# Crossing from a tiled attention-and-MoE front to a second MoE: the norm's steps and the last tile's scaling put ahead of side work, and the side steps of a quad's products dealt out by a table

## The chip, the core and the metric

One core of a Trainium2 chip runs the whole program in one launch. The metric is the device time of that core in microseconds (us); lower is better. The engines are TensorE (PE, with its weight loads shown apart as PEld), VectorE (DVE), ScalarE (ACT), GpSimd (POOL) and SyncE (SP), which only issues DMAs here. Each engine works through its own queue in order; semaphores let it wait for the others.

## What is computed

Three stages follow each other, all in fp32:

```
kv = einsum('bhsd,bhse->bhde', k, v);  out = einsum('bhsd,bhde->bhse', q, kv)   # B=4, H=8, S=576, D=64
x  = out / rms(out) * g_norm                       -> x [2304, 512]
h  = x @ w_in [512, 1024];  solu = h * softmax(h);  ln = (solu - mean) / std * g_ln
x  = ln @ w_out [1024, 512]                                                     # first MoE
y  = ((x @ w_a [512, 1536]) * (x @ w_b)) @ w_out2 [1536, 512]                   # second MoE
```

## The kernel before

**Front part.** The 2304 tokens are 18 tiles of 128. For a tile `i` the first MoE runs these steps: `hp` (24 matmuls into `ph`), `hm` (maximum, DVE), `he` (exponential, ACT), `hs` (SoLU, DVE, line 461), `hq` (squares, ACT, line 469), `hn` (the norm: a small tensor `nmu` on POOL, nine 128x1 steps on DVE from line 478 on, and for the last two tiles the scaling of `so` on ACT, line 486), `lt`/`lh`/`ll` (transposes on PE, line 495; their high part on ACT and low part on DVE), `yp`/`yk` (the product with `w_out`, 24 matmuls into `x2p`, and its copy by ACT to DRAM, `x2d`). The order is written out by hand in strings such as `LATER`, and `run(...)` emits it.

**Every fp32 operand is split** into a high and a low part (ACT casts the high part, DVE or POOL subtracts for the low part), and each product takes three matmuls: high by high, low by high, high by low.

**Second MoE.** Its tokens are three blocks `s` of 768, its hidden width six steps `j`, with `m` = 0 for `w_a` and `m` = 1 for `w_b`. `quad(j, s, m)` makes one 2x2 block product by seven smaller products (a Strassen-like scheme) in three PSUM banks, each product six matmuls of 384 columns. In the order of PE: the first (bank b1; ACT copies it out), the second (b2; DVE adds it into `22`, line 761), the third (b3; DVE adds it into `12`, line 765), then the last product of the quad before (`close_quad`), the fourth (b1), the fifth (b2) and the sixth (b3). The fifth may not write b2 before line 761 has read it, the sixth not b3 before line 765 has. After the fifth, the sixth and the closing product DVE adds once more (line 740); the closing product waits until the sixth product's add has read b3. With `m` = 1 the result is multiplied by that of `m` = 0 (line 751, mostly on POOL) and sent to DRAM (`gd`).

**Side work.** Operands for later quads are prepared between the products. `quad` takes a list `side` of steps, and after the first, second, third, fourth, fifth and sixth product `tick` emits some of them; before, `ceil(steps left / ticks left)` each time. `w_narrow` has ten steps (the absolute values on ACT, a clamp for each half on DVE, line 67, shifts, signs, lows, the next fetch), `w_sums` four (POOL or DVE), `w_split` four (cast, subtract, cast, subtract), `w2_sums` five, `x_steps` its casts and subtractions. In the last step `j` = 5 the quads run in the order of s = 1, 2, 0, and further steps (`then(t1=..., t6=...)`) are emitted at named ticks, after the side steps of that tick: loads of `gd` into `ga`, `te` and `gw`, loads of the last weights (`wo`), and their splits (`half`, `g_first`). After these come nine `out_pair` calls, the last matrix product.

**The crossing.** Tile 16 runs `LATER` with the first quad's operand splits (`side`, from `x_split`) put in between; tile 17 follows by hand. `w_split(0)` makes the first weight operands, `quad(0, 0, 0)` runs, then tile 17's transposes, the last `y_product` calls, and `quad(0, 0, 1)`. `w_sums(1)` runs on POOL.

Of the kernel before, what the change touches and what calls it, by code (L numbers as in the profile page):

```python
# [41 lines left out]
hp hm xt+1 op+2 lt0-1 lt1-1 lh0-1 lh1-1 ll0-1 ll1-1 xh+1 xl+1 he os+2 yp yk hs hq om+2 kp kk qt+3  # L42
qk+3 LQ yp yk hn MM E E BP BP ox+2 LK
"""


def split(nc, hi, lo, src, eng=None):
# [53 lines left out]
def tile_attention_moe(ctx, tc, q, k, v, g_norm, w_in, w_out, g_ln, w_a, w_b, w_out2, out):  # L101
    nc = tc.nc
# [442 lines left out]
    WA11, WA12, WS3, WA22, WS1, WS2, WS4 = range(7)  # L545
    XB11, XT1, XT2, XB21, XB22, XT3, XT4 = range(7)
# [178 lines left out]
    def quad(j, s, m, side=()):  # L725

        w, x = ws2[2 * j + m], xs2[s]
        side = list(side)
        ticks = [6]

        def tick():

            for _ in range(-(-len(side) // ticks[0])):
                side.pop(0)()
            for f in delayed.pop(7 - ticks[0], ()):
                f()
            ticks[0] -= 1

        def add(t, ps):
            nc.vector.tensor_tensor(out=t, in0=ps, in1=t, op=ALU.add)  # L740

        if m == 0:
            a_of[j, s] = {
                n: p2["a"].tile([P, TH], F32, tag=f"a{n}", name=f"a{n}") for n in (11, 12, 21, 22)
            }
        a = a_of[j, s]
        t = a if m == 0 else {n: p2["b"].tile([P, TH], F32, tag=f"b{n}", name=f"b{n}") for n in (12, 21, 22)}

        def times(n, by, eng):

            eng.tensor_tensor(out=a[n], in0=by, in1=a[n], op=ALU.mult)  # L751
            at_ = (11, 12, 21, 22).index(n)
            nc.sync.dma_start(out=gd[s][:, at_, :, j], in_=a[n].rearrange("p (m t) -> p m t", t=P))

        b1 = bank()
        product(b1, w, x, WA11, XB11, True, False)
        nc.scalar.copy(t[21], b1)
        tick()
        b2 = bank()
        product(b2, w, x, WS1, XT1, True, False)  # L760
        nc.vector.tensor_tensor(out=t[22], in0=b2, in1=t[21], op=ALU.add)  # L761
        tick()
        b3 = bank()
        product(b3, w, x, WS2, XT2, True, False)
        nc.vector.tensor_tensor(out=t[12], in0=b3, in1=t[21], op=ALU.add)
        close_quad()
        tick()
        product(b1, w, x, WA12, XB21, False, True)
        if m == 0:
            nc.scalar.copy(a[11], b1)  # L770
        else:
            times(11, b1, nc.vector)
        tick()
        product(b2, w, x, WS4, XB22, False, True)
        add(t[12], b2)
        if m:
            times(12, t[12], nc.gpsimd)
        tick()
        product(b3, w, x, WS3, XT3, False, False)
        add(t[22], b3)  # L780
        if m:
            times(22, t[22], nc.gpsimd)
        tick()

        def close():
            product(b3, w, x, WA22, XT4, False, True)
            add(t[21], b3)
            if m:
                times(21, t[21], nc.vector if (j, s) == (NJ - 1, 0) else nc.gpsimd)

        open_quad.append(close)
# [197 lines left out]
    def load_gl(_):  # L989
# [10 lines left out]
        lt0=lambda i: l_turn(i, 0), lt1=lambda i: l_turn(i, 1),  # L1000
        lh0=lambda i: l_hi(i, 0), lh1=lambda i: l_hi(i, 1),
        ll0=lambda i: l_lo(i, 0), ll1=lambda i: l_lo(i, 1),
# [3 lines left out]
    def run(order, i=0):  # L1006
        for token in order.split():
            name, _, at_ = token.replace("-", "+-").partition("+")
            if 0 <= i + int(at_ or 0) < NTILE:
                acts[name](i + int(at_ or 0))  # L1010
# [8 lines left out]
    def all_of(steps):  # L1019
        for f in steps:  # L1020
            f()
# [25 lines left out]
    i = NTILE - 2  # L1047
    side = [f for n in ORDER for f in x_split(0, n, lambda n=n: xf[n])]
    at_ = LATER.split().index("hn")
    run(" ".join(LATER.split()[:at_]), i)  # L1050
    all_of(side[:2])
    run("hn", i)
    all_of(w_sums(0))
    all_of(side[2:8])
    run(" ".join(LATER.split()[at_ + 1:]), i)
# [10 lines left out]
    p2["a"] = pool_r("a", 2, ab)  # L1066
    p2["b"] = pool_r("b", 1, ab)
    run("lt0-1 lt1-1 lh0-1 lh1-1 ll0-1 ll1-1", i)
    all_of(w_split(0, nc.vector))
    all_of(side[10:])  # L1070
    run("hs", i)
    while pend:
        y_product(0)
        y_keep(0)
    banks["pool"] = ps_t
    xf, sums = x_begin(1)
    quad(0, 0, 0, [lambda: run("hq", i), lambda: None, lambda: run("hn", i)])
    run("lt0 lt1 lh0 lh1 ll0 ll1", i)
    all_of(w_sums(1))
    all_of(sums)  # L1080
    all_of(w_split(1, nc.vector))
# [83 lines left out]
    def wl(n, place_, i, eng=nc.sync):  # L1165
        return lambda: wo_load(n, *place_[2 * i:2 * i + 2], eng)

    def half(n, part, eng=nc.vector):
        return hi_lo(wo2, n, eng, part)

    def gl_(n, c):
        return lambda: g_load(0, n, c, te[:, 2] if n == XT3 else None)
# [15 lines left out]
    for n, k in ((XB11, 0), (XT1, 1)):  # L1188
# [2 lines left out]
    most, last = slice(0, NJ - 1), slice(NJ - 1, NJ)  # L1191
    early, late_ = g_first(most), g_first(last)
    then(
        t1=[gl_(XB11, most), gl_(XT3, most)], t4=[gl_(XB22, most), gl_(XB21, most)], t6=early[:3],
    )
    quad(j, 1, 0)
    then(t1=early[3:4], t2=early[4:6], t3=early[6:7], t4=early[7:8], t5=early[8:10])
# [3 lines left out]
    )  # L1201
    quad(j, 2, 0)
    then(
        t2=half(WA11, 0), t3=[wl(WS2, w1, 2), *late_[:4]], t4=half(WA11, 1), t5=late_[4:8], t6=late_[8:],
    )
    quad(j, 2, 1)
    then(
        t1=half(WS1, 0), t2=half(WS1, 1), t3=[second_place], t4=[wl(WA12, w2, 0, nc.scalar), *half(WS2, 0)],
        t5=[wl(WS4, w2, 1, nc.scalar), *half(WS2, 1)], t6=[wl(WS3, w2, 2, nc.scalar), *g_split(0, XT2, lambda: te[:, 1])],
    )  # L1210
    quad(j, 0, 0)
# [39 lines left out]
    side = []  # L1251
# [49 lines left out]
```

## Time and profile before

| | us |
|---|---|
| median of three runs (lowest, highest) | 700.51 (699.49, 701.65) |
| the profiled execution's own time | 702.19 |
| its span in the trace | 700.1 |
| PE busy in the span | 665.7 |
| DVE, POOL, ACT busy | 519.6, 302.8, 284.1 |

The span is what the trace covers; the rest of the execution's time (2.1 us) lies around it. Times in rows are counted from the span's start. The front part lasts until about 283, the quads from there to about 572, the `out_pair` calls to the end.

### The profile page before, as it was taken

How to read it: one execution, taken by the hardware profiler on the slowest of the kernel's cores; microseconds unless marked ns; L12 is line 12 of the kernel's file. 1: busy time of each engine (PE TensorE's matmuls, PEld its weight loads, DVE VectorE, ACT ScalarE, POOL GpSimd, SP SyncE). 2: the span in 40 equal slices, each digit the busy share in tenths (PEclk: the TensorE clock that was granted, in tenths of full speed). 3: DMA queues.
4: the chain of work that ended last, by engine and by line, in shares of the span. 5: the costliest groups of instructions: out<-in, count | busy, mean ns of one | idle time of the engine just before them, and what ended most of it. 6: DMA issues, size and time to landing. Idle time of an engine off the chain costs nothing.

```text
span 700.1 us, 12578 instructions
## 1 busy us (share of the span) xinstructions
PE 665.7 (95%) x4710; PEld 633.0 (90%) x4710; DVE 519.6 (74%) x930; ACT 284.1 (41%) x491; POOL 302.8 (43%) x446
## 2 busy tenths in 40 slices
PE   1699999999999999999999999999999999999998
PEld 1577798999999998899999999999998899999998
DVE  3889977676688776779656867577656779987883
ACT  2558854544455346543331122212212445443431
POOL 2588776677666311113654467444672140000000
PEclk9899999999999999999999999999999999999999
DMA  9998645645542502342344336544334694654521
GB/s 248 316 248 234 184 127 156 168 127 149 178 127 76 167 16 68 106 136 81 111 149 136 118 106 187 177 136 142 112 95 129 221 313 139 190 146 130 150 76 61
DMA packets 107132, 103.84 MB, mean 148 GB/s; under 512 B 25280, under 2 KB 94400, under 8 KB 107072
## 3 DMA queue, kind: packets, MB, share of 16 engines
q1 hardware_dynamic: 101024, 94.40, 46.3%
q10 hardware_dynamic: 6048, 8.65, 3.7%
q8 instruction: 37, 0.61, 0.4%
q14 instruction: 23, 0.19, 0.1%
HBM read 71.05 MB, written 31.98 MB: 147 GB/s over the span
## 4 chain that ended last, share of the span: by engine, by line
PE 76%; DVE 9%; issue 5%; POOL 4%; DMA 3%; ACT 1%; SPq 1%; DVEq 0%; ACTq 0%; POOLq 0%
PE pw L710 26%; PE pq L881 18%; PE x2p L527 5%; PE x2p L525 5%; PE x2p L526 5%; PE ph L438 4%; PE ph L440 4%; PE ph L439 4%; PE ltp L495 2%; PE po L376 2%; DMA vs<-in_v_dram 1%; POOL a L751 1%; DMA wo<-w2d 1%; DMA gw<-gd 1%; PE xtp L413 1%
## 5 line engine op out<-in xcount | busy, mean ns | idle before, releaser
L751 POOL TENSOR_TENSOR a<-b,a 128x384 f32<-128x384 f32 x53 | 63.3, 1208 | 127.2 <-DVE b L740 126.2
L710 PE MATMUL pw<-xh,wh 128*128 128x384 f32 x336 | 114.3, 340 | 2.6 <-DVE b L761 1.6
L710 PE MATMUL pw<-xh,wl 128*128 128x384 f32 x336 | 112.7, 335 | 0.0
L710 PE MATMUL pw<-xl,wh 128*128 128x384 f32 x336 | 112.6, 335 | 0.0
L710 PE MATMUL pw<-x,wh 128*128 128x384 f32 x336 | 85.8, 336 | 0.9 <-DVE b L740 0.6
L525 PE MATMUL x2p<-lh,woh 128*128 128x256 f32 x288 | 82.6, 287 | 0.3 <-ACT lh L505 0.2
L526 PE MATMUL x2p<-ll,woh 128*128 128x256 f32 x288 | 80.6, 280 | 0.8 <-DVE ll L508 0.8
L527 PE MATMUL x2p<-lh,wol 128*128 128x256 f32 x288 | 80.6, 280 | 0.5 <-DVE wol L50 0.5
L710 PEld LDWEIGHTS pw<-xh,wh 128*128 128x128 f32 x336 | 63.1, 188 | 7.1 <-DVE b L761 2.3
L710 PEld LDWEIGHTS pw<-xl,wh 128*128 128x128 f32 x336 | 63.1, 188 | 0.0
L710 PEld LDWEIGHTS pw<-xh,wl 128*128 128x128 f32 x336 | 63.1, 188 | 0.0
L710 PEld LDWEIGHTS pw<-x,wh 128*128 128x128 f32 x336 | 60.5, 188 | 1.8 <-DVE b L740 0.9
L438 PE MATMUL ph<-wih,xh 128*128 128x512 f32 x144 | 56.9, 395 | 0.8 <-DVE so L461 0.8
L881 PE MATMUL pq<-wo,gh 128*128 128x256 f32 x336 | 57.7, 276 | 0.0
L440 PE MATMUL ph<-wih,xl 128*128 128x512 f32 x144 | 56.3, 391 | 1.2 <-DVE xl L423 1.2
L439 PE MATMUL ph<-wil,xh 128*128 128x512 f32 x144 | 56.3, 391 | 0.4 <-DVE wil L50 0.4
L710 PE MATMUL pw<-x,wl 128*128 128x384 f32 x168 | 56.2, 335 | 0.0
L527 PEld LDWEIGHTS x2p<-lh,wol 128*128 128x128 f32 x288 | 54.6, 190 | 0.9 <-DVE wol L50 0.9
L526 PEld LDWEIGHTS x2p<-ll,woh 128*128 128x128 f32 x288 | 54.2, 188 | 1.2 <-DVE ll L508 1.2
L525 PEld LDWEIGHTS x2p<-lh,woh 128*128 128x128 f32 x288 | 54.2, 188 | 0.9 <-ACT lh L505 0.5
L881 PE MATMUL pq<-wo,gw 128*128 128x256 f32 x450 | 53.1, 276 | 0.0
L67 POOL TENSOR_SCALAR nu<-nu 128x512 f32<-128x512 f32 x23 | 44.7, 1955 | 17.1 <-ACT nu L62 16.1
(158 smaller groups left out, 1536.0 us busy)
## 6 DMA issues: line engine op xcount, KB each, us to landing
gd<-a SPq DMA_DIRECT2D x72, 192.0 KB, 2.0
ring<-in_moe_w_out_dram SPq DMA_DIRECT2D x20, 512.0 KB, 5.4
gl<-gd SPq DMA_DIRECT2D x14, 384.0 KB, 3.5
gw<-gd SPq DMA_DIRECT2D x12, 384.0 KB, 3.2
ring<-in_moe_w_in_dram SPq DMA_DIRECT2D x8, 512.0 KB, 7.3
qs<-in_q_dram SPq DMA_DIRECT2D x16, 256.0 KB, 6.5
x2d<-x2s ACTq DMA_DIRECT2D x32, 128.0 KB, 1.8
st<-in_moe_w_a_dram SPq DMA_DIRECT2D x8, 512.0 KB, 4.3
```

The source lines that it names most:

```text
L67: eng.tensor_scalar(out=u, in0=u, scalar1=2.0 ** -15, scalar2=122879.9921875, op0=ALU.max, op1=ALU.min)
L376: nc.tensor.matmul(po[a:a + n, 2 * hp:2 * hp + 2, :], qT[i][:, hp, a:a + n], kvb[b % 3][:, hp, :], start=True, stop=True,)
L438: nc.tensor.matmul(ph[:, n, :], xh[:, c, :], wh, start=(c == 0), stop=False)
L439: nc.tensor.matmul(ph[:, n, :], xh[:, c, :], wl, start=False, stop=False)
L440: nc.tensor.matmul(ph[:, n, :], xl[:, c, :], wh, start=False, stop=(c == NK - 1))
L495: nc.tensor.transpose(pt[:, m, :], hs_[i]["so"][:, f * P:(f + 1) * P], ident)
L525: nc.tensor.matmul(pa, wh[:, cs], lh[:, f, :], start=(f == 0), stop=False)
L526: nc.tensor.matmul(pa, wh[:, cs], ll[:, f, :], start=False, stop=False)
L527: nc.tensor.matmul(pa, wl[:, cs], lh[:, f, :], start=False, stop=(f == NF1 - 1))
L710: nc.tensor.matmul(out, wt_[:, wn, c], xt_[xn][:, c], start=first and c == n == 0, stop=c == 1 and n == 2, skip_group_check=not first,)
L751: eng.tensor_tensor(out=a[n], in0=by, in1=a[n], op=ALU.mult)
L881: nc.tensor.matmul(ps, xt_[:, c], wt_[:, c], start=first and c == n == 0, stop=c == NJ - 1 and n == 2, skip_group_check=not first,)
```

## The change

It has three parts.

First, in the crossing, tile 16's `hn` is emitted before the first operand split instead of behind it; tile 17's `hs` comes before `w_split(0)` and the last four operand splits instead of after them; its `hq` comes after the first of the remaining `yp yk` instead of after the first quad's first product; and its transposes and their splits come after the fifth product of `quad(0, 0, 0)` instead of after the whole quad.

Second, a table `DEAL` says for 13 kinds of quad, by (s, m, number of side steps), how many steps follow each of the six products.

Third, in the steps `then(...)` of the last `j`, some are moved by one tick.

```diff
+DEAL = {
+    (0, 0, 6): "121011",
+    (0, 1, 8): "312020",
...
+    (2, 1, 4): "111001",
+    (0, 0, 4): "102100",
+    (0, 1, 10): "113212",
+    (1, 0, 8): "321011",
+    (1, 1, 10): "033202",
...
         ticks = [6]
+        deal = DEAL.get((s, m, len(side)))
...
-            for _ in range(-(-len(side) // ticks[0])):
+            for _ in range(-(-len(side) // ticks[0]) if deal is None else int(deal[6 - ticks[0]])):
                 side.pop(0)()
...
     run(" ".join(LATER.split()[:at_]), i)
+    run("hn", i)
     all_of(side[:2])
-    run("hn", i)
     all_of(w_sums(0))
...
     run("lt0-1 lt1-1 lh0-1 lh1-1 ll0-1 ll1-1", i)
+    run("hs", i)
     all_of(w_split(0, nc.vector))
     all_of(side[10:])
-    run("hs", i)
+    run("yp yk hq", i)
     while pend:
...
-    quad(0, 0, 0, [lambda: run("hq", i), lambda: None, lambda: run("hn", i)])
-    run("lt0 lt1 lh0 lh1 ll0 ll1", i)
+    none = [lambda: None]
+    quad(0, 0, 0, [lambda: run("hn", i), *3 * none, lambda: run("lt0 lt1 lh0 lh1 ll0 ll1", i), *none])
     all_of(w_sums(1))
...
-        t1=[gl_(XB11, most), gl_(XT3, most)], t4=[gl_(XB22, most), gl_(XB21, most)], t6=early[:3],
+        t1=[gl_(XB11, most), gl_(XT3, most)], t3=[gl_(XB22, most), gl_(XB21, most)], t6=early[:3],
...
-        t2=half(WA11, 0), t3=[wl(WS2, w1, 2), *late_[:4]], t4=half(WA11, 1), t5=late_[4:8], t6=late_[8:],
+        t3=[wl(WS2, w1, 2), *half(WA11, 0), *late_[:4]], t4=[*half(WA11, 1), *late_[4:8]], t6=late_[8:],
...
-        t1=half(WS1, 0), t2=half(WS1, 1), t3=[second_place], t4=[wl(WA12, w2, 0, nc.scalar), *half(WS2, 0)],
+        t2=half(WS1, 0), t3=[second_place, *half(WS1, 1)], t4=[wl(WA12, w2, 0, nc.scalar), *half(WS2, 0)],
```

No instruction is added or taken away. The queues differ at these places above all.

DVE in the crossing, before: behind the last operand splits (`wl`, `xl`) come tile 17's SoLU (`rs`, `so`), then the first quad's adds of the second and third product (`a<-pw,a`), then the norm's small steps (`va` to `nmu`), the adds of the fifth and sixth product, and the low parts `ll` of the transposes.

```order
L552 TENSOR_TENSOR wl_3611<-w0s,wh_3610 128x768 [waits Activation_49]
L552 TENSOR_TENSOR xl_3385<-xf,xh_3378 128x768 [waits Activation_49]
L552 TENSOR_TENSOR xl_3386<-xf,xh_3379 128x768 [waits Activation_49]
L457 TENSOR_SCALAR rs<-se 128x1
L461 SCALAR_TENSOR_TENSOR so,su<-ph,rs,e 128x1024 [waits DVE_49]
L761 TENSOR_TENSOR a_3751<-pw,a_3750 128x384 [waits PE_49,Activation_49]
L765 TENSOR_TENSOR a_3749<-pw,a_3750 128x384 [waits PE_49]
L478 TENSOR_SCALAR va<-vs 128x1 [waits Activation_49]
L485 TENSOR_TENSOR nmu<-nmu,y_l 128x1 [waits DVE_49,Pool_49]
L740 TENSOR_TENSOR a_3749<-pw,a_3749 128x384 [waits PE_49]
L740 TENSOR_TENSOR a_3751<-pw,a_3751 128x384 [waits PE_49]
L508 TENSOR_TENSOR ll<-ltp,lh 128x4x128 [waits Activation_49] x2
```

The same place on DVE after the change (line numbers are 15 or 16 higher):

```order
L472 TENSOR_SCALAR rs<-se 128x1
L476 SCALAR_TENSOR_TENSOR so,su<-ph,rs,e 128x1024 [waits DVE_49]
L567 TENSOR_TENSOR wl_3617<-w0s,wh_3616 128x768 [waits Activation_49]
L567 TENSOR_TENSOR xl_3385<-xf,xh_3378 128x768 [waits Activation_49]
L567 TENSOR_TENSOR xl_3386<-xf,xh_3379 128x768 [waits Activation_49]
L493 TENSOR_SCALAR va<-vs 128x1 [waits Activation_49]
L500 TENSOR_TENSOR nmu<-nmu,y_l 128x1 [waits DVE_49,Pool_49]
L777 TENSOR_TENSOR a_3753<-pw,a_3752 128x384 [waits PE_49,Activation_49]
L781 TENSOR_TENSOR a_3751<-pw,a_3752 128x384 [waits PE_49]
L756 TENSOR_TENSOR a_3751<-pw,a_3751 128x384 [waits DVE_49,PE_49]
L523 TENSOR_TENSOR ll<-ltp,lh 128x4x128 [waits Activation_49] x2
L756 TENSOR_TENSOR a_3753<-pw,a_3753 128x384 [waits PE_49]
```

The SoLU moved ahead of the operand splits, the norm's steps ahead of the quad's first add, and the low parts ahead of the sixth product's add. On PE the eight transposes moved ahead of the sixth product, and nothing else there moved in the whole program.

DVE in `quad(1, 1, 1)`, before; `quad(j, 1, 1)` and `quad(j, 0, 1)` of j = 1 to 4 read alike. `b<-pw,b` of line 761 and 765 are the adds of the second and third product, line 740 the later adds, 67 to 93 the steps of `w_narrow`, 751 the multiplication of the fourth product.

```order
L67 TENSOR_SCALAR st<-st 128x512 [waits Activation_49]
L761 TENSOR_TENSOR b_4555<-pw,b_4554 128x384 [waits PE_49]
L67 TENSOR_SCALAR st<-st 128x512 [waits Activation_49]
L82 TENSOR_SCALAR st<-st 128x512 [waits DVE_49]
L765 TENSOR_TENSOR b_4553<-pw,b_4554 128x384 [waits PE_49]
L740 TENSOR_TENSOR a_4487<-pw,a_4487 128x384 [waits DMAHW4_49,PE_49]
...
L93 SCALAR_TENSOR_TENSOR st<-st 128x512 [waits DVE_49]
L740 TENSOR_TENSOR b_4553<-pw,b_4553 128x384 [waits PE_49]
L93 SCALAR_TENSOR_TENSOR st<-st 128x512 [waits DVE_49]
L740 TENSOR_TENSOR b_4555<-pw,b_4555 128x384 [waits PE_49]
```

After the change:

```order
L777 TENSOR_TENSOR b_4555<-pw,b_4554 128x384 [waits PE_49,Activation_49]
L82 TENSOR_SCALAR st<-st 128x512 [waits Activation_49] x2
L781 TENSOR_TENSOR b_4553<-pw,b_4554 128x384 [waits PE_49]
L756 TENSOR_TENSOR a_4487<-pw,a_4487 128x384 [waits DMAHW4_49,PE_49]
L97 TENSOR_SCALAR st<-st 128x512 [waits DVE_49] x2
...
L108 SCALAR_TENSOR_TENSOR st<-st 128x512 [waits DVE_49]
L756 TENSOR_TENSOR b_4553<-pw,b_4553 128x384 [waits PE_49]
L756 TENSOR_TENSOR b_4555<-pw,b_4555 128x384 [waits PE_49]
L108 SCALAR_TENSOR_TENSOR st<-st 128x512 [waits DVE_49]
```

The second product's add moved ahead of the first clamp, both clamps now stand ahead of the third product's add, the first shift behind it, and the last low behind the sixth product's add.

DVE in `quad(5, 2, 1)`, before (`wo`: the low part of a half of the weights `WA11`):

```order
L761 TENSOR_TENSOR b_6206<-pw,b_6205 128x384 [waits PE_49,Activation_49]
L552 TENSOR_TENSOR wo_6175<-wo_6175 128x768 [waits DMAHW3_49,Activation_49]
L765 TENSOR_TENSOR b_6204<-pw,b_6205 128x384 [waits PE_49]
L740 TENSOR_TENSOR a_6131<-pw,a_6131 128x384 [waits DMAHW4_49,PE_49]
L552 TENSOR_TENSOR te<-te,ga 128x128 [waits DMAHW5_49,DMAHW4_49]
```

After the change:

```order
L777 TENSOR_TENSOR b_6206<-pw,b_6205 128x384 [waits PE_49,Activation_49]
L781 TENSOR_TENSOR b_6204<-pw,b_6205 128x384 [waits PE_49]
L756 TENSOR_TENSOR a_6131<-pw,a_6131 128x384 [waits DMAHW4_49,PE_49]
L567 TENSOR_TENSOR wo_6175<-wo_6175 128x768 [waits DMAHW3_49,Activation_49]
L567 TENSOR_TENSOR te<-te,ga 128x128 [waits DMAHW5_49,DMAHW4_49]
```

The weights' subtraction moved behind two adds. On POOL, in `quad(j, 2, 1)`, the second subtraction of `w_split` moved behind the multiplications of the fifth and sixth product. SP's queue keeps its order everywhere.

## Rows read from the trace of the kernel before

**Rows 1.** Page, first part: busy us (share), instructions, of the matmuls.

```profile
PE 665.7 (95%) x4710; PEld 633.0 (90%) x4710; DVE 519.6 (74%) x930; ACT 284.1 (41%) x491; POOL 302.8 (43%) x446
```

**Rows 2.** Timeline, PEld: start, us, line, tile, count, [idle before it and releaser].

```profile
271.16 0.86 PEld L495 LDWEIGHTS ltp<-ident,so 128*128 128x128 f32 x8 [1.07 <-ACT so L486]
290.70 0.85 PEld L495 LDWEIGHTS ltp<-ident,so 128*128 128x128 f32 x8 [1.19 <-ACT so L486]
292.03 0.19 PEld L525 LDWEIGHTS x2p<-lh,woh 128*128 128x128 f32 x1 [0.47 <-ACT lh L505]
292.76 0.19 PEld L526 LDWEIGHTS x2p<-ll,woh 128*128 128x128 f32 x1 [0.54 <-DVE ll L508]
317.91 0.19 PEld L710 LDWEIGHTS pw<-xh,wh 128*128 128x128 f32 x1 [0.45 <-DVE a L765]
...
347.87 0.19 PEld L710 LDWEIGHTS pw<-xh,wh 128*128 128x128 f32 x1 [0.27 <-DVE a L765]
369.34 0.19 PEld L710 LDWEIGHTS pw<-xh,wh 128*128 128x128 f32 x1 [0.69 <-DVE b L761]
375.08 0.19 PEld L710 LDWEIGHTS pw<-xh,wh 128*128 128x128 f32 x1 [0.46 <-DVE b L740]
...
507.89 0.19 PEld L710 LDWEIGHTS pw<-xh,wh 128*128 128x128 f32 x1 [0.47 <-DVE b L740]
533.36 0.19 PEld L710 LDWEIGHTS pw<-xh,wh 128*128 128x128 f32 x1 [1.58 <-DVE b L761]
...
549.74 0.30 PEld L710 LDWEIGHTS pw<-x,wh 128*128 128x128 f32 x2 [0.62 <-DVE b L765]
554.77 0.30 PEld L710 LDWEIGHTS pw<-x,wh 128*128 128x128 f32 x2 [0.90 <-DVE b L740]
557.33 0.19 PEld L710 LDWEIGHTS pw<-xh,wh 128*128 128x128 f32 x1 [0.52 <-DVE a L761]
558.66 0.19 PEld L710 LDWEIGHTS pw<-xh,wh 128*128 128x128 f32 x1 [0.34 <-DVE a L765]
```

**Rows 3.** Timeline, PE: the product of 533.36 itself.

```profile
533.36 0.44 PE L710 MATMUL pw<-xh,wh 128*128 128x384 f32 x1 [1.26 <-DVE b L761]
```

**Rows 4.** Timeline in the crossing: DVE, ACT and POOL.

```profile
266.81 1.00 DVE L552 TENSOR_TENSOR xl<-xf,xh 128x768 fp32r<-128x768 f32 x1 [3.14 <-ACT xh L587]
269.87 1.24 ACT L486 ACTIVATE so<-so,nmu,y_l 128x1024 f32<-128x1024 f32 x1 [3.09 <-DVE nmu L485]
280.89 1.82 DVE L552 TENSOR_TENSOR xl<-xf,xh 128x768 fp32r<-128x768 f32 x2
283.01 1.28 DVE L461 SCALAR_TENSOR_TENSOR so<-ph,rs,e 128x1024 f32<-128x1024 f32 x1
285.38 2.26 POOL L552 TENSOR_TENSOR w0s<-w0s 128x256 f32<-128x256 f32 x3
```

**Rows 5.** Timeline in `quad(2, 1, 1)`: DVE's two clamps and last add, POOL's subtractions.

```profile
411.71 1.37 DVE L67 TENSOR_SCALAR st<-st 128x512 f32<-128x512 f32 x1 [2.46 <-ACT st L62]
413.47 0.41 DVE L67 TENSOR_SCALAR st<-st 128x512 f32<-128x512 f32 x1
418.74 0.55 DVE L740 TENSOR_TENSOR b<-pw,b 128x384 f32<-128x384 f32 x1
408.57 4.22 POOL L552 TENSOR_TENSOR wl<-st,wh 128x1024 fp32r<-128x1024 f32 x2 [0.18 <-ACT wh L688]
```

**Rows 6.** Timeline around `quad(5, 1, 1)`, DVE and SP; last, the page's part on DMA issues.

```profile
532.01 0.83 DVE L552 TENSOR_TENSOR te<-gw,te 128x640 f32<-128x640 f32 x1 [1.17 <-DMA gw<-gd]
525.98 1.01 SPq L829 DMA_DIRECT2D gw<-gd  x2
gw<-gd SPq DMA_DIRECT2D x12, 384.0 KB, 3.2
```

**Rows 7.** Timeline, DVE, in `quad(5, 2, 1)` and at the end of `quad(5, 0, 0)`.

```profile
548.25 0.96 DVE L552 TENSOR_TENSOR wo<-wo 128x768 fp32r<-128x768 f32 x1 [2.31 <-ACT wo L869]
561.56 0.55 DVE L740 TENSOR_TENSOR a<-pw,a 128x384 f32<-128x384 f32 x1
```

More of the change, by code (lines that the diff above doesn't have):

```diff
@@ L44 @@
 """
+DEAL = {
+    (0, 0, 6): "121011",
+    (0, 1, 8): "312020",
+    (1, 0, 9): "231111",
+    (1, 1, 9): "122112",
+    (2, 0, 8): "221012",
+    (2, 1, 4): "111001",
[3 more added lines that the diff above has]
+    (1, 1, 10): "033202",
+    (2, 0, 4): "111010",
+    (0, 0, 5): "003011",
+    (2, 0, 9): "233010",
+}
 def split(nc, hi, lo, src, eng=None):
```

## The prediction, made before the changed kernel ran

> **What bounds the kernel now.** I read the page first, for the busy time of each engine: PE computes 95% of the span, DVE 74%, ACT and POOL less than half [rows 1]. PE works through its queue in order and the change gives it no instruction less, so only its idle time can be won. The second view was the timeline of PEld, from the end of the front part on, filtered for rows with a wait in brackets. It is a short list: the waits from 271 to the end [rows 2]. The reader is to see three things there: no wait stands after 558.66, so the `out_pair` calls lose nothing; two places hold most of the sum, the crossing (271 to 293) and the last `j` (533 to 559); and between them one pattern comes back every six quads.
>
> A wait of PEld is a little longer than what PE loses, because PE still finishes the product ahead. At 533.36 PEld waited 1.58 and PE 1.26 [rows 2, 3]; I take the mean, 1.42, which is 0.9 of the first, and count 0.9 of every wait of PEld.
>
> The third view was the timeline of all engines around each of these places, to see what the releasing instruction had been late for [rows 4 to 7].
>
> The pattern also gives PE's pace: from 375.08 to 507.89 three periods pass, 44.27 each [rows 2]. A period is six quads of 42 matmuls; less its wait (0.47) that is 0.174 a matmul, 1.04 for a product of six, 3.12 for three.
>
> **The change, part by part.** Nothing is added or removed, so each cost is a wait that goes or one that comes.
>
> *The crossing, tile 16.* ACT's scaling of `so` starts at 269.87 after 3.09 idle; it waited for the norm's steps, which filled DVE from the end of the first `xl` (266.81 + 1.00) to that start, 2.1 long. They stood behind that `xl`, and DVE idled 3.14 before it, waiting for ACT's cast [rows 4]. Ahead of the cast the steps run in that idle time, and the transposes no longer wait 1.07 [rows 2]: gain 1.07 x 0.9 = 0.96. The `xl` behind them finds its idle time shortened; the first quad needs it more than 10 us later.
>
> *The crossing, tile 17.* The SoLU at 283.01 stood behind two `xl` (1.82) and the two `wl` [rows 4], the norm behind two adds of the quad, the transposes behind the quad; PE waited 1.19 + 0.47 + 0.54 [rows 2]. Now all of it moves ahead, and the transposes have a sixth product, 1.04, between them and the products that need them: gain 2.2 x 0.9 = 1.98. Together the crossing gives 2.94 at most.
>
> *What this makes late.* POOL's `w0s` sums (three in 2.26, so 0.75 each, four in all) run behind POOL's part of the norm, which waits for the SoLU. They ran from 285.38 at the latest [rows 4], behind DVE's low parts; with the SoLU earlier they run beside `wl` and `xl`. What POOL can do to DVE is seen in `quad(2, 1, 1)`: a clamp took 1.37, and ended at 413.08 as POOL's subtractions did at 412.79; the next took 0.41 [rows 5]. In the crossing DVE would be held for up to 4 x 0.75 = 3.0. Queued behind are the norm's 2.1 and then the first quad's add of the second product, on which the fifth product waits. I take half of the 3.0 as held, half of that as hidden by the two products in between (2 x 1.04 on PE): 0.75 lost, bounds 0 and 1.5. The crossing: 2.94 - 0.75 = **2.2** (1.4 to 3.0).
>
> The Trainium skill has the rule behind this (SBUF — State Buffer, Who interferes with whom): a VectorE instruction with two SBUF inputs, or in a mode with two ports, contends with a GpSimd instruction that reads SBUF, and the one that issues second is blocked for the whole of the first. The clamp agrees with it [rows 5]; the subtractions in the crossing have two inputs and so would be held. By that rule the sum is the one below, and without any holding it would be 8.4.
>
> *Dealing, `quad(j, 1, 1)`.* The clamps of `w_narrow` came in the first tick: the held clamp stood ahead of the second product's add, and all that followed was late, to the last add at 418.74 (0.55). The next quad's closing product waits for that add; this is the pattern of 0.46 to 0.47 at 375.08 to 507.89, four times, and the wait of 0.69 at 369.34 is for the add itself [rows 2, 5]. In the new order that add goes first and the last low of `w_narrow` goes behind the last add, which therefore ends at least 0.47 earlier. Gain (0.69 + 4 x 0.465) x 0.9 = **2.3**. The price: both clamps now stand ahead of the third product's add, which the sixth product waits for. The first clamp ends at 413.08 when POOL does, the second 0.41 and the add 0.55 later, at 414.0. The sixth product starts four products before the closing one was wanted: 419.33 less its wait 0.47 less 4 x 1.04, 414.7. So 0.7 is in hand and I price the move at nothing; without that cover each 0.1 costs 0.4 over four quads.
>
> *Dealing, `quad(1, 0, 0)`.* Its weight subtraction moves behind adds; the wait of 0.27 at 347.87 goes: **0.24**. The waits that line 765 makes at 317.91 (0.45) and two smaller ones like it lie in quads whose order hardly moves: nothing, at most 3 x 0.45 x 0.9 = 1.2 [rows 2].
>
> *The wait at 533.36* [rows 2]. DVE stood at `te<-gw`, waiting for the load of `gw`; SP issued it at 525.98, and it ended 6.0 later at 532.0, against 3.2 for the median of such loads [rows 6]. The edit moves the subtraction by a tick, but SP's queue is unchanged, so the load must come earlier by itself. In `quad(5, 2, ...)` and its like POOL's second subtraction (4.22 / 2 = 2.1 [rows 5]) moves behind two multiplications of the quad, whose results SP sends and the loads follow; so the load can start up to about 2 earlier and may land anywhere from 529.2 (issue + 3.2) to 532.0. Half or more of the delay must go for most of the wait to go: **1.1**, bounds 0 and 1.42.
>
> *The end of `j` = 5.* Waits 0.62, 0.90, 0.52 and 0.34 [rows 2]: 2.38 x 0.9 = 2.14. Each is for an add that stood behind a weight subtraction like that of 548.25, 0.96 long and itself waiting 2.31 for ACT [rows 7]. These move behind adds. But DVE works almost without a break from 548.25 to 561.56 + 0.55 = 562.1; about 1.0 of two adds moves ahead of it, and it then ends at 561.1. The closing product of `quad(5, 0, 0)` would be wanted, PE having won 2.1, at 558.66 + 1.04 - 2.14 + 3 x 1.04 = 560.7: a new wait of about 0.35. Left: **1.8** (1.3 to 2.1).
>
> Sum: 2.2 + 2.3 + 0.24 + 1.1 + 1.8 = **7.6**. The profiled execution took 702.19 (its span 700.1 and 2.1 around it): it goes to 694.6. It lay 1.68 above the median of the runs, 700.51, so on that scale the prediction is **692.9**.
>
> **The rivals.**
> *The loads set the pace of the last quads.* The load at 533.36 lands as late as before (SP's order speaks for it), and what DVE then has to make up costs half of the 1.8. Gain 7.6 - 1.1 - 0.9 = 5.6: 694.9.
> *POOL holds DVE more than I count.* The crossing loses 0.75 more, and in the four quads DVE is held beyond the 0.7 by 0.35 each, 1.4: gain 5.4, 695.1. For it: the clamp of 1.37. Against it: in the quads the pair of POOL itself does not move.
> *All waits go,* the three of line 765 too, and no new one comes: 2.94 + 2.3 + 0.24 + 1.42 + 2.14 + 1.2 = 10.2: 690.2. Against it: DVE has no idle time left at the end.
> *The dealing does nothing,* its waits only move to the next add, and the crossing alone counts: 2.2, 698.3. Against it: the adds that are waited for move ahead of what held them, and behind them stands slack.
> *Slower:* in `quad(j, 1, 1)` the third product's add is late behind both clamps, because ACT's absolute values or POOL's pair end later than now. It decides when it eats the rest (7.6 - 2.3 = 5.3) and 2.1 more: 7.4 over four quads, 1.85 each beyond the 0.7, the add ending at 416.6 or later: 702.6 and up. Nothing in the rows delays it by so much.
>
> **How the numbers follow.** Gain of 6 to 9 as summed, 0.62; the loads 0.15; POOL 0.08; all waits gone 0.08; dealing nothing 0.05; slower 0.02. The range goes from all waits gone, 690.2, to 696.5: the bounds of my terms added at their worst (1.4 + 2.3 + 0 + 0 + 1.3 = 5.0, 695.5) and 1 for the spread of the runs. A measurement of this kernel tells about 0.3%, 2.1, from no change. The first four cases lie beyond that, 0.93; the fifth lies at its edge and counts as same, 0.05; slower 0.02.
>
> **What would show it.** In the new profile: PEld's wait of 1.07 and those of the transposes gone, and at most one of 0 to 1.5 at the fifth product of `quad(0, 0, 0)`, with DVE's `wl` or `xl` longer beside POOL's `w0s`; no wait of 0.46 at the closing products after `quad(j, 1, 1)`; `te<-gw` of `quad(5, 1, 1)` earlier against PE, and a wait below 0.5 there; one small wait at the close of `quad(5, 0, 0)`. The prediction is wrong if waits of the same size turn up at the sixth product of `quad(j, 1, 1)` (its slack was thinner than 0.7), if the 1.58 stays, or if waits come where there were none before, in the quads of the other table entries.

## The result and the profile after

The changed kernel took 691.71 us, the median of four runs (690.78 to 693.09), against 700.35 of the kernel before (699.49 to 701.65): a ratio of 0.9877, 95% interval 0.9854 to 0.99, or 8.6 us less (7.0 to 10.2). Forecast were 692.9 and a range from 690.2 to 696.5. The profiled execution took 691.45, its span 689.6; before it was 702.19 and 700.1.

The first part of the page (busy time, share, instructions) says little: PE does the same 4710 matmuls, its busy time is 662.6 against 665.7 in [rows 1], and its share rises because the span shrinks.

```profile
PE 662.6 (96%) x4710; PEld 636.0 (92%) x4710; DVE 522.7 (76%) x930; ACT 283.6 (41%) x491; POOL 307.2 (45%) x446
```

The view that tells the change is the timeline of PEld, filtered for rows with a wait. Where [rows 2] show fourteen rows (the whole list of the kernel before, from 255 on and of waits of 0.15 or more, adds up to 11.48 us with the six that stand between them), after the change one is left:

```profile
552.32 0.19 PEld L725 LDWEIGHTS pw<-xh,wh 128*128 128x128 f32 x1 [0.59 <-DVE a L756]
```

It is the closing product of `quad(5, 0, 0)`, waiting for DVE's last add. 11.48 - 0.59 = 10.89, and the profiled execution fell by 702.19 - 691.45 = 10.74: between these two executions the list is the whole difference (by the spans, 700.1 - 689.6 = 10.5, within 0.4).

In the crossing (timeline of ACT, DVE and POOL, then PE and PEld at the transposes; compare [rows 4]) the SoLU now starts at 277.55, 5.5 earlier, and the norm's `so` at 285.74, ahead of the transposes, which wait for nothing:

```profile
277.55 1.28 DVE L476 SCALAR_TENSOR_TENSOR so<-ph,rs,e 128x1024 f32<-128x1024 f32 x1
278.76 2.09 DVE L567 TENSOR_TENSOR wl<-w0s,wh 128x1024 fp32r<-128x1024 f32 x2
280.77 2.92 DVE L567 TENSOR_TENSOR xl<-xf,xh 128x768 fp32r<-128x768 f32 x2
...
285.65 0.56 DVE L777 TENSOR_TENSOR a<-pw,a 128x384 f32<-128x384 f32 x1
280.01 1.44 POOL L679 TENSOR_TENSOR w0s<-w0s 128x256 f32<-128x256 f32 x1
281.53 3.45 POOL L567 TENSOR_TENSOR w0s<-w0s 128x256 f32<-128x256 f32 x3
285.74 1.25 ACT L501 ACTIVATE so<-so,nmu,y_l 128x1024 f32<-128x1024 f32 x1 [0.59 <-DVE nmu L500]
286.34 0.19 PEld L725 LDWEIGHTS pw<-xh,wh 128*128 128x128 f32 x1
287.38 0.97 PEld L510 LDWEIGHTS ltp<-ident,so 128*128 128x128 f32 x8
```

The reader is to see POOL's sums beside DVE's subtractions. The two `xl` take 2.92 where they took 1.82, and POOL's three sums 3.45 where they took 2.26 [rows 4]: they hold each other. DVE loses 1.1 by it. The first add of the quad still ends at 286.21; the fifth product, which waits for it, starts one product (1.04) ahead of the transposes, at 286.5 by their PE row, and its first weight load goes 0.17 ahead of it, at 286.34. The holding is there, the wait is not, by 0.13.

In `quad(2, 1, 1)` (timeline of DVE, and POOL's subtractions; compare [rows 5]) the second product's add no longer stands behind a held clamp:

```profile
405.31 0.56 DVE L777 TENSOR_TENSOR b<-pw,b 128x384 f32<-128x384 f32 x1 [1.59 <-PE pw L725]
406.67 1.69 DVE L82 TENSOR_SCALAR st<-st 128x512 f32<-128x512 f32 x2 [0.80 <-ACT st L77]
408.28 0.55 DVE L781 TENSOR_TENSOR b<-pw,b 128x384 f32<-128x384 f32 x1
...
412.15 1.01 DVE L756 TENSOR_TENSOR b<-pw,b 128x384 f32<-128x384 f32 x2
403.52 4.22 POOL L567 TENSOR_TENSOR wl<-st,wh 128x1024 fp32r<-128x1024 f32 x2 [0.17 <-ACT wh L703]
409.03 0.19 PEld L725 LDWEIGHTS pw<-xh,wh 128*128 128x128 f32 x1
```

The clamps are still held until POOL ends at 407.74, and the third product's add, now behind both, ends at 408.83. The sixth product started at 409.20 and its first weight load at 409.03, so of the 0.7 in hand 0.37 were there by the product and 0.20 by its load.

Before the product that waited 1.58 (timeline of SP and DVE; compare [rows 6]) the load of `ga` is issued 3.6 ahead of that of `gw`, and `gw` is there 4.2 after its own issue, not 6.0:

```profile
515.23 0.44 SPq L845 DMA_DIRECT2D ga<-gd  x1
518.85 0.98 SPq L845 DMA_DIRECT2D gw<-gd  x2
523.06 0.82 DVE L567 TENSOR_TENSOR te<-gw,te 128x640 f32<-128x640 f32 x1 [1.04 <-DMA gw<-gd]
```

The kernel before issued `ga` at

```profile
524.18 0.43 SPq L829 DMA_DIRECT2D ga<-gd  x1
```

1.8 ahead of `gw` [rows 6]. DVE still waits 1.04 for `gw`, but the add behind it is done in time.

At the end of the last `j` (timeline of DVE, then POOL; compare [rows 7]) DVE works without a break, and the closing product's add comes last:

```profile
550.85 0.94 DVE L567 TENSOR_TENSOR wo<-wo 128x768 fp32r<-128x768 f32 x1
551.72 0.54 DVE L756 TENSOR_TENSOR a<-pw,a 128x384 f32<-128x384 f32 x1
552.19 0.94 DVE L567 TENSOR_TENSOR gw<-te,gw 128x768 fp32r<-128x768 f32 x1
552.26 4.39 POOL L567 TENSOR_TENSOR wo<-wo 128x768 fp32r<-128x768 f32 x2 [2.61 <-ACT wo L885]
```

### The profile page after: what moved, and what is told of

Its sections match the earlier page's. It is cut to its first block, busy times and chain, and to the rows that moved or that the text cites. A ratio compares the mean times of both kernels' runs of the same rounds, so it can differ in the third digit from the quotient of the medians.

```text
span 689.6 us, 12588 instructions
## 1 busy us (share of the span) xinstructions
PE 662.6 (96%) x4710; PEld 636.0 (92%) x4710; DVE 522.7 (76%) x930; ACT 283.6 (41%) x491; POOL 307.2 (45%) x446
## 4 chain that ended last, share of the span: by engine, by line
PE 89%; DVE 6%; DMA 1%; POOL 1%; SPq 1%; issue 1%; ACT 0%; DVEq 0%; POOLq 0%
PE pw L725 37%; PE pq L897 19%; PE x2p L542 5%; PE x2p L540 5%; PE x2p L541 5%; PE ph L455 4%; PE ph L453 4%; PE ph L454 4%; PE ltp L510 2%; PE po L391 2%; DMA vs<-in_v_dram 1%; PE kvp L357 1%; DVE so L476 1%; PE qtp L377 1%; DVE nm L461 1%
## 5 line engine op out<-in xcount | busy, mean ns | idle before, releaser
L767 POOL TENSOR_TENSOR a<-b,a 128x384 f32<-128x384 f32 x53 | 65.0, 1241 | 119.5 <-DVE b L756 119.5
L725 PE MATMUL pw<-xh,wh 128*128 128x384 f32 x336 | 112.8, 336 | 0.3 <-DVE a L756 0.3
```

What stands on the lines that cost most here:

```text
L725: nc.tensor.matmul(out, wt_[:, wn, c], xt_[xn][:, c], start=first and c == n == 0, stop=c == 1 and n == 2, skip_group_check=not first,)
```

## The experiments

The theory is that the span is a constant and the list: the time that PE needs, and each wait of PEld with its full length. In the two executions above the span less the list is 700.1 - 11.48 = 688.6 and 689.6 - 0.59 = 689.0. The constant is more than PE's need: ahead of 255, where the list begins, the kernel before has 31 more waits of PEld, 32.3 us with the 11.7 before its first weight load, and the change leaves that part of the program as it is. The first three kernels make one part of the change each, the fourth is the kernel before again.

**The crossing alone.** Its edit, in short:

```diff
+    run("hn", i)
     all_of(side[:2])
-    run("hn", i)
...
+    run("hs", i)
     all_of(w_split(0, nc.vector))
     all_of(side[10:])
-    run("hs", i)
+    run("yp yk hq", i)
...
+    quad(0, 0, 0, [lambda: run("hn", i), *3 * none, lambda: run("lt0 lt1 lh0 lh1 ll0 ll1", i), *none])
```

> The crossing's part alone: the norm's steps, the SoLU, the squares and the last tile's transposes moved as in the change, no table and no step of the last j moved. The theory (each wait of the weight loads is worth its full length, and the parts do not touch each other) expects the four waits of the crossing (1.07, 1.19, 0.47, 0.54) gone and no new one at the fifth product of quad(0, 0, 0), 3.2 us faster, about 697.1 where the kernel before takes 700.35; all the waits from 317 on stay as before. The rival of the prediction (POOL's sums hold DVE and cost PE 0.75) expects 698 and a wait of about 0.75 there. If the three small waits at line 765 and 761 (317.91, 325.52, 339.30 before) go here, they hang on the crossing; if they stay, on the table.

The runs took 697.0 (median) against 700.49, ratio 0.9945 (0.993 to 0.996), 3.9 us less (2.8 to 4.9). The four waits of the crossing are gone, and no new one stands before 314. The three small waits stay (0.45, 0.35, 0.26), so they hang on the table. The wait at 533 is there, shorter (0.95).

**The table alone.**

```diff
+        deal = DEAL.get((s, m, len(side)))
...
-            for _ in range(-(-len(side) // ticks[0])):
+            for _ in range(-(-len(side) // ticks[0]) if deal is None else int(deal[6 - ticks[0]])):
```

> The table alone, crossing and last j as before. The theory expects the waits of quad(j, 1, 1) (0.69 and four of 0.47), that of 0.27 and the three small ones (0.45, 0.34, 0.28) gone, and the wait of 1.58 at 533 as well, since the loads behind the quad (4, 2, 1) are issued earlier by the table's entry for a (2, 1) quad of 4 steps: 5.4 us faster, about 694.9. The rival (the wait of 1.58 goes by the moved tick of the loads in the last j) expects that wait to stay and 3.8, about 696.5. Both keep the crossing's 3.3 and the waits from 549 on (2.4).

The runs took 694.76, ratio 0.9911 (0.9895 to 0.9927), 6.2 us less (5.1 to 7.4). Between the crossing's waits and 547 the list is empty, and in the last `j` it is down to three rows, 1.13 where the kernel before has 2.38 [rows 2]:

```profile
547.69 0.30 PEld L725 LDWEIGHTS pw<-x,wh 128*128 128x128 f32 x2 [0.32 <-DVE b L756]
550.25 0.19 PEld L725 LDWEIGHTS pw<-xh,wh 128*128 128x128 f32 x1 [0.49 <-DVE a L777]
551.58 0.19 PEld L725 LDWEIGHTS pw<-xh,wh 128*128 128x128 f32 x1 [0.32 <-DVE a L781]
```

That was not expected: the theory had left the waits of the last `j` to the moved ticks. ACT's timeline shows where the other half went. The cast of the first weights there waits for a load, in the kernel before and with the table alone:

```profile
547.38 0.84 ACT L869 CAST wo<-wo 128x768 fp32r<-128x768 f32 x1 [2.57 <-DMA wo<-w2d]
```

```profile
540.32 0.84 ACT L885 CAST wo<-wo 128x768 fp32r<-128x768 f32 x1 [1.42 <-DMA wo<-w2d]
```

ACT issued that load 6.2 and 5.1 us earlier (541.15 and 535.24). With the crossing alone it took 5.2, and there too the waits are down, to 0.44 + 0.49 + 0.33 = 1.26 from 549 on. So it is not the table alone that takes them; the waits go with a load that takes one microsecond more or less.

**The moved ticks alone.**

```diff
-        t1=[gl_(XB11, most), gl_(XT3, most)], t4=[gl_(XB22, most), gl_(XB21, most)], t6=early[:3],
+        t1=[gl_(XB11, most), gl_(XT3, most)], t3=[gl_(XB22, most), gl_(XB21, most)], t6=early[:3],
...
-        t1=half(WS1, 0), t2=half(WS1, 1), t3=[second_place], t4=[wl(WA12, w2, 0, nc.scalar), *half(WS2, 0)],
+        t2=half(WS1, 0), t3=[second_place, *half(WS1, 1)], t4=[wl(WA12, w2, 0, nc.scalar), *half(WS2, 0)],
```

> The moved ticks of the last j alone. The theory expects the waits of 549.74, 554.77, 557.33 and 558.66 (2.38 in all) gone, one new wait of about 0.6 at the close of quad(5, 0, 0), and 1.58 at 533 unchanged: 1.8 us faster, about 698.5. The rival (the wait of 1.58 goes by the moved tick) expects 3.4, about 697. Should the late loads of 533 also make the steps behind them late, as one rival of the prediction had it, half of the 1.8 is lost.

The runs took 701.05, ratio 1.0003 (0.9991 to 1.0015, twelve runs): no gain. Both expectations miss. PEld's list at the end of this kernel's last `j`, and DVE and POOL there:

```profile
533.25 0.19 PEld L710 LDWEIGHTS pw<-xh,wh 128*128 128x128 f32 x1 [0.29 <-DVE b L761]
...
561.11 0.19 PEld L710 LDWEIGHTS pw<-xh,wh 128*128 128x128 f32 x1 [0.68 <-DVE a L740]
564.00 0.19 PEld L710 LDWEIGHTS pw<-xh,wh 128*128 128x128 f32 x1 [0.84 <-DVE b L761]
560.98 2.50 DVE L552 TENSOR_TENSOR gw<-te,gw 128x768 fp32r<-128x768 f32 x1
560.82 4.36 POOL L552 TENSOR_TENSOR wo<-wo 128x768 fp32r<-128x768 f32 x2 [2.38 <-PE pw L710]
```

The four waits from 549 on are gone, but two have come, 1.52 for 2.38. The second is a chance of order: POOL's subtraction started 0.16 ahead of DVE's `gw<-te,gw`, and DVE took 2.50 where it took 0.94 in the profile of the change, 0.07 ahead of POOL.

**The kernel before again.** No edit.

> The kernel before once more, unchanged, for a second profile: the theory expects the same list of waits within 0.1 each, that of 1.58 too, and a span of 698 to 700. If the load of gw took 6 us only by chance in the first profile, the wait at 533 is much shorter here.

It took 703.21, span 701.1, list 13.13; span less list 688.0. Not the same list: the wait at 533 was 1.93, and around `quad(1, 1, 1)` there were two more (0.53 at 355.04 and 0.48 at 359.64) and a longer one at the second product's add,

```profile
370.17 0.19 PEld L710 LDWEIGHTS pw<-xh,wh 128*128 128x128 f32 x1 [1.22 <-DVE b L761]
```

(0.69 in [rows 2]). Their cause stands on ACT's timeline: the absolute value waits for the raw weights, 2.10 here and 0.69 in the first profile of the kernel before.

```profile
353.07 0.66 ACT L62 ACTIVATE st<-st 128x512 f32<-128x512 f32 x1 [2.10 <-DMA st<-in_moe_w_a_dram]
```

The way from there to PEld is in the same timelines: DVE's clamp waits 1.87 for that absolute value, its adds and with them POOL's multiplications and subtractions come some 0.8 later (POOL's pair at 365.15, 364.32 in the first profile), and the next clamps and the add stand behind POOL. So the list of the kernel before changed by 1.65 us between two executions, with what its loads did, and the profile that the prediction started from was not its middle.

**Crossing and table, without the moved ticks.**

```diff
-        t1=[gl_(XB11, most), gl_(XT3, most)], t3=[gl_(XB22, most), gl_(XB21, most)], t6=early[:3],
+        t1=[gl_(XB11, most), gl_(XT3, most)], t4=[gl_(XB22, most), gl_(XB21, most)], t6=early[:3],
...
```

> The change without its moved ticks of the last j. With the crossing and the table alone having given ratios of 0.9945 and 0.9911, and their lists of waits having no entry in common, the theory (the span is 688.6 and the waits of the list) expects the three waits that the table alone left in the last j (0.32, 0.49, 0.32) and nothing else: a span of about 689.7 and a median near 691.5, as fast as the whole change within what can be told. The rival (the moved ticks are worth the 1.8 of the prediction) expects 693.5.

The runs took 691.86, ratio 0.9862 (0.9837 to 0.9887), span 689.2, list 0.22 + 0.50 + 0.32 = 1.04, with the load of `wo` taking 5.0. That is as fast as the whole change, as far as the interval tells, and with 1.04 left to win at most, the rival's 1.8 for the moved ticks is out.

**The change without one entry of the table.**

```diff
-    (2, 1, 4): "111001",
```

> The change without the table's entry for quad (2, 1) with 4 steps, so that POOL's second subtraction stands again ahead of the multiplications whose results are loaded back. The theory expects SP to issue the load of ga about 1.8 us later against PE, 1.8 instead of 3.6 ahead of that of gw, and gw to land later: a wait of 0.3 to 1.9 at the fifth quad's first add comes back (it was 1.58, 1.93, 0.95 and 0.29 in the four profiles without the table). The rival (the wait went by the moved tick, or by chance) expects none.

One execution took 692.78. `ga` was issued 1.8 ahead of `gw` again, as expected, but no wait came back at 533: `gw` was there before DVE wanted it, at most 6.2 after `ga`'s issue. The expectation missed, and the two runs at the end of this section take it up.

**A subtraction done twice in the crossing.** The kernel does one operand subtraction once more than it needs.

```diff
-    all_of(side[10:])
+    all_of([*side[10:], side[-1]])
```

> The change with the last operand subtraction of the crossing done twice, which puts 0.9 to 1.4 us more on DVE ahead of the norm's steps and of the first add of quad(0, 0, 0). In the profile of the change that add ended at 286.21 and the fifth product started at 286.50, so the theory expects a wait of 0.6 to 1.2 at the fifth product (and the transposes behind it no further wait). If the prediction's slack of about 1 held, the wait would be under 0.4.

One execution took 693.53. PEld, and DVE's three `xl`:

```profile
287.77 0.19 PEld L725 LDWEIGHTS pw<-xh,wh 128*128 128x128 f32 x1 [1.32 <-DVE a L777]
280.86 4.34 DVE L567 TENSOR_TENSOR xl<-xf,xh 128x768 fp32r<-128x768 f32 x3
```

4.34 - 2.92 = 1.42 more on DVE, 1.32 waited: the slack was 0.1, as the weight load at 286.34 had it, and not the 0.3 of the product. The path that the prediction feared is right (sums beside subtractions, the norm behind, then the add, then the fifth product); the change just stays on the good side of it.

**Two more steps ahead of the third product's add.**

```diff
-    (1, 1, 10): "033202",
+    (1, 1, 10): "053002",
```

> The change with two more steps of w_narrow, the shifts, ahead of the third product's add in quad(j, 1, 1): 0.75 us more on DVE before it. In the profile of the change that add ended at 408.83 in quad(2, 1, 1) and the sixth product started at 409.20, a slack of 0.37: the theory expects a wait of about 0.4 at the sixth product in four or more quads, 1.5 us or more in all. With the slack of 0.7 that the prediction gave, it would be 0.05 each and hardly seen.

One execution took 695.0. Waits of 1.42, 0.54, 0.52 and 0.53 at the sixth products, the last three alike; the first of them and one that stands for them:

```profile
366.68 0.19 PEld L725 LDWEIGHTS pw<-xh,wh 128*128 128x128 f32 x1 [1.42 <-DVE b L781]
410.91 0.19 PEld L725 LDWEIGHTS pw<-xh,wh 128*128 128x128 f32 x1 [0.54 <-DVE b L781]
```

0.75 more on DVE gave 0.53: a slack of 0.2, that of the weight load. The slower rival of the prediction is a real mechanism that starts 0.5 earlier than it said. In `j` = 1 it shows 0.9 more, and in the profiles of the two variants before it a wait of 0.97 and 0.79 stands at the same place, though the table's entry is the change's own. In both, ACT waited longer for the raw weights a quad before (up to 2.15 and 1.71, 0.83 in the profile of the change), so a late load makes the clamps late there, by the way that the kernel before had shown.

**The change with two more moves,** and beside it the change again:

```diff
-    (1, 1, 10): "033202",
+    (1, 1, 10): "014104",
...
+    ws2_ = half(WS2, 1)
...
-        t5=[wl(WS4, w2, 1, nc.scalar), *half(WS2, 1)],
+        t5=[wl(WS4, w2, 1, nc.scalar), ws2_[0]],
...
-        t1=[next_load(XB11)], t2=[next_load(XT1)],
+        t1=[next_load(XB11)], t2=[next_load(XT1), ws2_[1]],
```

> The change with two more moves: in quad(5, 0, 0) the last weight subtraction goes from between the fifth and the sixth product's add to behind the next quad's second product's add; and in quad(j, 1, 1) both clamps go behind the third product's add (table entry 014104), since their slack there was 0.37 and in two profiles of variants j = 1 waited 0.8 to 1.0 at that add. The theory expects no wait at the close of quad(5, 0, 0) (0.59 in the profile of the change), none at the sixth products of quad(j, 1, 1), and a median 0.6 to 1.2 below the change run beside it, 0.1 to 0.2%. It fails if the clamps, now later, push the last adds of quad(j, 1, 1) past the next closing product (their slack was 0.23), which would show as four waits there.

> The changed kernel again, beside the run before this one on the same chip. The theory expects a median of 691 to 692.5 and a list with the wait of 0.59 at the close of quad(5, 0, 0), or with 0.84 at the next quad's second product as well where POOL's weight subtraction starts just ahead of DVE's; and now and then one of up to 1 at the sixth product of quad(1, 1, 1).

The runs took 691.31 (0.9849, 0.9833 to 0.9864) with the two moves and 691.9 (0.9858, 0.9842 to 0.9874) for the change, on the same chip: not to be told apart. With the moves the wait of 0.59 at the close is gone, and one of the same size stands in the next quad: its sixth product waits for the third product's add, which is behind the moved subtraction, held by POOL. A wait of 0.24 is new in `j` = 1:

```profile
372.07 0.30 PEld L725 LDWEIGHTS pw<-x,wh 128*128 128x128 f32 x2 [0.24 <-DVE a L777]
555.90 0.19 PEld L725 LDWEIGHTS pw<-xh,wh 128*128 128x128 f32 x1 [0.59 <-DVE b L781]
553.10 2.27 DVE L567 TENSOR_TENSOR wo<-wo 128x768 fp32r<-128x768 f32 x1
```

The change again shows the chance of order that the moved ticks alone had shown. Here POOL started 0.10 ahead of DVE; in the first profile of the change DVE started 0.07 ahead of POOL, and the list had no second row:

```profile
551.98 0.19 PEld L725 LDWEIGHTS pw<-xh,wh 128*128 128x128 f32 x1 [0.59 <-DVE a L756]
554.93 0.19 PEld L725 LDWEIGHTS pw<-xh,wh 128*128 128x128 f32 x1 [0.89 <-DVE b L777]
551.86 2.55 DVE L567 TENSOR_TENSOR gw<-te,gw 128x768 fp32r<-128x768 f32 x1
551.76 4.36 POOL L567 TENSOR_TENSOR wo<-wo 128x768 fp32r<-128x768 f32 x2 [2.44 <-PE pw L725]
```

**The one entry alone, and the earlier loads alone,** each put on the kernel before:

```diff
+DEAL = {
+    (2, 1, 4): "111001",
+}
```

> The kernel before with one entry of the table alone, quad (2, 1) with 4 steps. The theory expects the load of ga issued 3.6 ahead of that of gw (1.8 without the entry) and the wait at 533 gone; all other waits as before, a span of about 699. If the wait stays, other entries of the table took it away.

One execution took 702.07. `ga` at 524.20, `gw` at 527.81, 3.6 apart, and no wait at 533. The entry alone is enough there. The time itself was no better, since `quad(1, 0, 0)` waited 1.64 (0.27 in [rows 2]). That wait is the entry's own: `quad(0, 2, 1)` has four side steps too, the `w_sums`, and the entry puts POOL's last sum behind two multiplications, so that ACT's cast of the weights, and DVE's subtraction and add behind it, come late:

```profile
344.85 1.99 POOL L755 TENSOR_TENSOR a<-b,a 128x384 f32<-128x384 f32 x2
346.80 0.74 POOL L555 TENSOR_TENSOR st<-st 128x256 f32<-128x256 f32 x1
347.57 1.78 ACT L691 CAST wh<-st 128x1024 fp32r<-128x1024 f32 x2 [3.18 <-POOL st L555]
```

The kernel before did all four sums ahead of those multiplications, and the cast started 3.2 earlier, 2.0 of it beyond the shift that is told below:

```profile
344.36 1.78 ACT L688 CAST wh<-st 128x1024 fp32r<-128x1024 f32 x2 [1.12 <-POOL st L552]
```

In the change POOL's sum comes as late, but the entry (0, 0, 4) puts DVE's subtraction behind the add that is waited for, and no wait is left. This execution also stood 1.18 later before the entry could matter, at the last of the three small waits (340.48 against 339.30); why stays open.

```diff
-        t1=[gl_(XB11, most), gl_(XT3, most)], t4=[gl_(XB22, most), gl_(XB21, most)], t6=early[:3],
+        t1=[gl_(XB11, most), gl_(XT3, most)], t3=[gl_(XB22, most), gl_(XB21, most)], t6=early[:3],
```

> The kernel before with the loads of gw emitted one tick earlier and nothing else. SP's queue then reads as before, so the theory expects no effect: ga 1.8 ahead of gw, gw there 6.2 to 8.2 after the issue of ga as in the runs so far, and a wait of 0.3 to 1.9 at 533. The rival (the moved tick shortens the load) expects gw there within 6.6 and a wait under 0.3, as in the two kernels that had the moved tick without the entry.

One execution took 703.21. `ga` 1.8 ahead of `gw`, `gw` there 6.95 after `ga`, the wait

```profile
534.36 0.19 PEld L710 LDWEIGHTS pw<-xh,wh 128*128 128x128 f32 x1 [0.70 <-DVE b L761]
```

The rival, by which the moved tick shortens the load, is not borne out. Over the kernels without the entry the load needed 6.2 or less to 8.2 from the issue of `ga`, and the wait was 0 to 1.93; in the eight with it the load needed 7.3 to 8.0 and the wait was never there. Why one load needs 6 and another 8 stays open.

## Why the prediction came out right, step by step

Its mechanisms were right but for the end of `j` = 5, and most terms were too small. By the lists of the two first profiles (without one wait of 0.15), forecast and found:

| term | forecast | waits gone less come |
|---|---|---|
| crossing | 2.2 | 1.07 + 1.19 + 0.47 + 0.54 = 3.27 |
| `quad(j, 1, 1)` | 2.3 | 2.56 |
| `quad(1, 0, 0)` | 0.24 | 0.27 |
| wait at 533, with 0.20 behind it | 1.1 | 1.78 |
| end of `j` = 5 | 1.8 | 2.38 - 0.59 = 1.79 |
| small waits at 317.91 and two others | 0 | 1.07 |
| sum | 7.6 | 10.74 |

**The price of a wait.** I counted 0.9 of PEld's wait from one row pair [rows 2, 3]. In thirteen of the fourteen profiles span less list lies between 688.0 and 689.2 (the one with the single entry gives 689.7), while the list goes from 0.59 to 13.13. A straight line through the fourteen rises by 1.00 us of span for 1 us of list (standard error 0.03), and by 0.98 without that one: a wait costs its full length, or nearly. That alone is about 1 us.

**The crossing's new wait (0.75).** The holding came as reckoned, 1.1 on DVE against 1.5, and it was hidden, by 0.13. All of the term was there; its loss was not. The Trainium skill's rule (SBUF — State Buffer, Who interferes with whom) held: of two instructions that want the SBUF ports which VectorE and GpSimd share, the one issued first blocks the other for its whole length. The trace agrees with both sides of it in one place, 0.07 and 0.10 apart (0.94 and 2.55 for the same subtraction), and with its exception for an instruction with at most one SBUF input: the add with one input in PSUM took 0.56 at 405.31, in the middle of POOL's subtractions.

**`quad(j, 1, 1)`.** Right, with a slack of 0.2 where 0.7 was read. The clamps were not the fault: the add ended 1.09 after POOL did (408.83 - 407.74), and the prediction had reckoned 1.2 (414.0 - 412.79). What was off is where PE stands. The 414.7 that I had reckoned back for the sixth product holds a wait for this very add, of the six that [rows 2] leave out:

```profile
414.73 0.19 PEld L710 LDWEIGHTS pw<-xh,wh 128*128 128x128 f32 x1 [0.15 <-DVE b L765]
```

Without it the load was wanted 1.79 after POOL's end (414.58 - 412.79); in the changed kernel it came 1.29 after (409.03 - 407.74). Against PE, POOL's pair moved 0.5 later, and the prediction had held that it does not move. Why it moved, no run shows.

**The wait at 533.** The cause was right (POOL's second subtraction moves behind the multiplications), one link was wrong: I let the load of `gw` start earlier. It starts as before; `ga` and `te` ahead of it start 1.8 and 1.1 earlier and are out of the way. The one entry alone shows it.

**The end of `j` = 5.** The sum was right for this pair of profiles (1.79 for 1.8), but by luck: as a gain of the moved ticks it failed. Alone they gain nothing (1.0003), and the change without them is as fast (691.86). What they take away is 2.3 to 2.4 where the load of `wo` takes 6.2 to 6.3, and 1.0 to 1.3 where it takes 5.0 to 5.2; what they leave in its place is 0.59, or 1.28 to 1.52 where POOL starts first. I had read the size from the kernel before, whose load is late, and counted all of it for the ticks. The load goes with the rest of the change: in the nine profiles with the whole crossing, or with the table or all but one entry of it, it took 5.0 to 5.2, and in the five without (the kernel before twice, the one entry, the earlier loads, the moved ticks alone) 5.9 to 6.3. Each part alone had it fast, in one profile each; by what way stays open. The new wait at the close of `quad(5, 0, 0)` was forecast at its place, at 0.35 (its own terms give 561.1 - 560.7 = 0.4), and came at 0.59.

**The small waits.** Held for untouched; the table alone takes them, the crossing alone doesn't.

**The rival that came nearest** is that all waits go, 690.2; the measured 691.71 lies between it and the forecast. That the median fell by 8.6 and not by 10.7 is for the most part the profile of before: it ran 1.8 above the median of its runs, and a later execution of the same kernel took 703.21. So it is in part luck that the forecast came within 1.2: the terms were 3.1 short of the lists that they were read from, and 2.1 of these the medians did not show. By span less list (688.6) and the 2 us around the span, the median runs had lists of about 9.8 and 1.1; that is an estimate.

## What to carry to other kernels

Where one engine is busy nearly all the time, list the waits of its queue and add them up. Here the sum was, at nearly full price, the ceiling of what reordering could give in the stretch that the list covers, and each row named the instruction to move; the waits ahead of 255 were not in it. Take that list from two or three executions, since waits that hang on loads change: here by 1.65 in all between two executions of one kernel, as much as a term that one reckons. An entry that takes one wait away can make another (1.64 for the one entry alone), so a table is to be tried whole. Once the list was near zero, further moves only shifted the last wait: the two tried here changed its place and not the time.

## What the runs showed of the hardware that had not been expected

The time of a subtraction on DVE with two SBUF operands hung on 0.1 us: 0.94 where it started 0.07 ahead of POOL's, 2.55 where POOL was 0.10 ahead, with 0.89 us of PE behind it. Six profiles have the moved ticks of the last `j` and the pair in this order: DVE was 0.07 and 0.02 ahead in two (0.94 each), POOL 0.10 to 0.28 ahead in four (2.38 to 2.55). In the crossing both sides lost (2.92 for 1.82 on DVE, 3.45 for 2.26 on POOL), as their instructions alternate. And the same loads, issued in the same order, took from 6.2 or less to 8.2 us over the kernels without the entry (`gw`, from the issue of `ga`) and from 5.0 to 6.3 (`wo`), the latter sorted by kernel: 5.9 or more in those with neither the crossing nor the table, 5.2 or less in the others.
